# Sliding-window attention with a feed-forward behind it: the opening as one written list for all engines, keys loaded once a step

## The chip, the cores and the metric

The kernel runs on one core of a Trainium2 chip. The metric is the device time of the one launch in microseconds; lower is better.

## The reference

Attention over 4 batches, 8 heads, 768 tokens and 64 dimensions; a query sees the 8 global tokens and the 96 tokens up to itself, with a bias by distance. The attention's output, as 3072 tokens of 512 features, goes through a gated feed-forward without a nonlinearity.

```python
scores = scale * np.matmul(q, k.transpose(0, 1, 3, 2))
...
keep = is_global | is_local
dist = np.where(is_global & ~is_local, float(n_local), np.abs(rel))
bias = -slopes[:, None, None] * dist[None, :, :]
scores = np.where(keep, scores + bias, -1e9)
a = softmax(scores)
x = np.matmul(a, v)
...
a = x @ w1                      # 512 -> 1024
b = x @ w2
h = a * b @ w3                  # 1024 -> 1024
return h @ w_out                # 1024 -> 512
```

The inputs are float32; the weights come as 64-bit floats, which the kernel converts itself.

## The kernel before

*Weights.* `w3 @ w_out` is folded into one 1024x512 matrix on the chip: `fold(f, k)` (L135) adds one of 8 x 8 products, each two TensorE instructions, to the product for row block f. The result is split into a high and a low part (`wh` at L145, `wl` at L148). `w1` and `w2` are split likewise, 16 pieces (`w12`, L549; high part at L124, low part at L132). The 40 pieces of 512 KB (16 of `w3t`, 8 of `w_out`, 16 of `w1` and `w2`) come as 64-bit words into raw buffers (`stage`, `stage_xh`, `stage_xl`, `raws`) and are made to 32-bit words by three VectorE operations each (L56, L58, L60). `weights(...)` (L99) issues the loads of one or two pieces on SP's queue and converts them interleaved.

*Attention.* A step s is 128 queries of one batch and all heads, 24 steps, six to a batch. `load_keys` (L393) brings four overlapping windows of keys, 96 + 32 local and 8 global ones for each block of 32 queries, and the queries; `load_values` (L400) the values. Both tiles have one buffer. `scores` (L415) makes 32 small matmuls into the PSUM tile `sc`; `rows` (L428) takes the row maximum on VectorE (L435) and the exponential with its sum on ScalarE (L436); `probabilities` (L445) scales (L455 on ScalarE in steps 0 to 3, L458 on VectorE later) and transposes in 32x32 blocks (L461) into `pt`; `values` (L463) multiplies `pt` with the values by 64 small matmuls (32 in the first step of a batch) into the first 128 columns of `sc`; `tokens` (L502) splits the result into `xh` and `xl` (L65, L66).

*Feed-forward.* `run` (L150) is a generator for one unit of tokens, 256 for the first two units and 512 for the other five. It yields after about six matmuls, a slice; a unit of 512 tokens has 48 slices, one of 256 has 24. `gh` and `gl`, the gated product in two parts, use the buffers that hold `wo` and the raw pieces before.

*Order.* TensorE follows the program's order everywhere. The opening, `first_steps` (L515: the weights, steps 0 to 3 and the first slices), gives VectorE and SP their order too, while ScalarE's order there is the planner's. From step 4 on TensorE and ScalarE follow the program and VectorE and SP the planner. There a step is `visit(s)` (L493: `values(s - 1)`, `scores(s)`, and the loads), the rows with one slice behind each of the four query blocks, `tokens(s - 1)`, two slices, `probabilities(s)` and the other slices, 12 from step 8 on. A unit of 512 tokens is put behind the waiting work by `tokens`.

Of the kernel before, what the change touches and what calls it, by code (L numbers as in the profile page):

```python
# [45 lines left out]


def convert(nc, pieces):


    for dst, raw, src in pieces:
        nc.sync.dma_start(out=dst if src.dtype == F32 else raw, in_=src.bitcast(I32))
    pieces = [(dst, raw.rearrange("p (n t) -> p n t", t=2)) for dst, raw, src in pieces if src.dtype != F32]

    for dst, w in pieces:
        nc.vector.tensor_scalar(out=dst, in0=w[:, :, 1], scalar1=3, scalar2=0x3FFFFFF8, op0=ALU.logical_shift_left, op1=ALU.bitwise_and)  # L56
    for dst, w in pieces:
        nc.vector.scalar_tensor_tensor(out=dst, in0=w[:, :, 1], scalar=-0x40000000, in1=dst, op0=ALU.bitwise_and, op1=ALU.bitwise_or)  # L58
    for dst, w in pieces:
        nc.vector.scalar_tensor_tensor(out=dst, in0=w[:, :, 0], scalar=29, in1=dst, op0=ALU.logical_shift_right, op1=ALU.bitwise_or)  # L60
# [8 lines left out]
class FeedForward:  # L69
# [25 lines left out]
    def next(self, ring, slots):
        self.turn[ring] += 1
        return slots[(self.turn[ring] - 1) % len(slots)]

    def weights(self, *names):  # L99


        pieces, fresh = [], []
        for kind, *at in names:
            if kind == "w":
                f, n = divmod(at[0], 2)

                raw = self.stage[{3: 0, 5: 2, 6: 0}[f] + n] if f in (3, 5, 6) else self.raws[:, n]
                dst, src = self.t3s[:, at[0] % 4], self.src[n][f]
                fresh.append((n, f, dst.bitcast(F32).rearrange("p (i m) -> p i m", i=NCC)))
            elif kind == "o":  # L110
                dst, src = self.wo[:, at[0]], self.w_out[at[0]]
            else:
                f, z = at
                dst = self.mp.tile([P, PC], I32, tag=self.next(0, "agagoo"), name=f"t3_{f}_{z}")
                src = self.w3t[f, :, z * PC:(z + 1) * PC]
                self.t3[f, z] = dst
            if kind != "w":
                raw = self.next(1, self.stage + self.first)
            pieces.append((dst, raw, src))
# [533 lines left out]
```

## Time and profile before

| what | us |
|---|---|
| median of three runs | 596.34 (594.66 to 597.28) |
| the profiled execution | 594.8 |
| its span, first to last instruction | 592.9 |
[...]

The span is what the trace shows; the rest of the profiled execution's time lies around it. Busy times count an engine's instructions; consecutive matmuls overlap, so the time of a run of matmuls is read from the pitch between starts and not from the duration of one.

### The profile page before, as it was taken

Reading aid. Unit: us, or ns where it says so; the run is one execution under the profiler, and the core shown is the slowest. Engines: PE = TensorE matmul, PEld = TensorE weight load, DVE = VectorE, ACT = ScalarE, POOL = GpSimd, SP = SyncE. Lnnn points to the kernel's source line nnn. Section 1 sums busy time; section 2 is a strip of 40 time slices with the busy share of each in tenths; the row PEclk is TensorE's granted clock in tenths of the full one; section 3 lists DMA queues with packets and bytes.
Section 4 is the critical chain, followed back from the end, with each engine's and each line's share of the span. In section 5 each row is a group of like instructions: output and inputs, shape, how many; then the busy total and the mean of one; then the engine's idle time right before and its main releaser. Section 6 shows DMA issues by size and latency. Waiting matters only on the chain.

```text
span 592.9 us, 14620 instructions
## 1 busy us (share of the span) xinstructions
PE 538.7 (91%) x6400; PEld 423.2 (71%) x6400; DVE 273.6 (46%) x788; ACT 187.0 (32%) x591; POOL 2.9 (0%) x20
## 2 busy tenths in 40 slices
PE   2959597979999799999999998999979999999995
PEld 0424254977998588887877787888867878888884
DVE  7759687885354343533355413535233454112200
ACT  2032533544243243233324322433232343112210
POOL 1000000000000000000000000000000000000000
PEclk9979978989999899999999999999999999999999
DMA  8678554732144242134213322231342131100011
GB/s 288 250 278 295 221 192 161 271 130 72 49 141 167 92 130 92 44 106 148 86 46 128 132 94 108 73 112 48 119 166 66 65 130 38 55 18 1 1 37 40
DMA packets 17881, 69.52 MB, mean 117 GB/s; under 512 B 1936, under 2 KB 3984, under 8 KB 15248
## 3 DMA queue, kind: packets, MB, share of 16 engines
q1 hardware_dynamic: 17808, 68.49, 32.5%
q8 instruction: 52, 0.85, 0.6%
q14 instruction: 21, 0.17, 0.1%
HBM read 62.20 MB, written 6.29 MB: 116 GB/s over the span
## 4 chain that ended last, share of the span: by engine, by line
PE 74%; DVE 13%; ACT 5%; DMA 4%; issue 2%; SPq 1%; ACTq 0%; DVEq 0%
PE m L163 14%; PE m L162 14%; PE m L164 14%; PE o L179 7%; PE o L181 7%; PE o L180 7%; PE sc L478 6%; PE sc L426 4%; ACT pr L436 2%; PE w L143 2%; DVE pt L461 1%; ACT pr L455 1%; DVE t3s L58 1%; DMA stage<-w 1%; DMA stage_xh<-w_out 1%
## 5 line engine op out<-in xcount | busy, mean ns | idle before, releaser
L436 ACT ACTIVATE pr<-pr,mx 128x136 f32<-128x136 f32 (+2 forms) x192 | 74.2, 388 | 83.0 <-DVE mx L435 83.0
L162 PE MATMUL m<-xh,w1h 128*128 128x512 f32 (+1 forms) x224 | 82.4, 368 | 6.4 <-ACT xh L65 6.4
L172 DVE TENSOR_TENSOR g<-m,a 128x512 f32<-128x512 f32 x48 | 33.0, 688 | 110.7 <-PE m L164 110.7
L163 PE MATMUL m<-xl,w1h 128*128 128x512 f32 (+1 forms) x224 | 81.7, 365 | 2.1 <-DVE xl L66 2.1
L164 PE MATMUL m<-xh,w1l 128*128 128x512 f32 (+1 forms) x224 | 81.1, 362 | 0.0
L162 PE MATMUL m<-xh,w2h 128*128 128x512 f32 (+1 forms) x224 | 80.7, 360 | 0.0
L164 PE MATMUL m<-xh,w2l 128*128 128x512 f32 (+1 forms) x224 | 80.4, 359 | 0.0
L163 PE MATMUL m<-xl,w2h 128*128 128x512 f32 (+1 forms) x224 | 80.3, 359 | 0.0
L143 PE MATMUL w<-wo,t 128*128 128x512 f32 x128 | 61.2, 636 | 17.8 <-DVE wo L60 17.4
L179 PE MATMUL o<-wh,gh 128*128 128x512 f32 x192 | 76.0, 396 | 0.3 <-ACT gh L65 0.3
L181 PE MATMUL o<-wh,gl 128*128 128x512 f32 x192 | 74.9, 390 | 0.0
L180 PE MATMUL o<-wl,gh 128*128 128x512 f32 x192 | 74.8, 390 | 0.0
L65 ACT ACTIVATE gh<-g 128x512 fp32r<-128x512 f32 x48 | 30.3, 632 | 125.6 <-DVE g L172 125.6
L143 PEld LDWEIGHTS w<-wo,t 128*128 128x128 f32 x128 | 25.5, 205 | 51.0 <-issue 28.0
L435 DVE CUSTOM_DVE_ANT_0 pr<-sc,biasw 128x136 f32<-128x136 f32 x160 | 37.0, 295 | 50.5 <-PE sc L426 50.5
L478 PEld LDWEIGHTS sc<-pt,vr 32*64 32x64 f32 x2816 | 40.8, 140 | 24.8 <-DVE pt L461 17.5
L478 PE MATMUL sc<-pt,vr 32*64 32x32 f32 (+3 forms) x2816 | 44.5, 260 | 14.7 <-DVE pt L461 14.7
L162 PEld LDWEIGHTS m<-xh,w1h 128*128 128x128 f32 x224 | 42.6, 190 | 16.1 <-ACT xh L65 8.1
L163 PEld LDWEIGHTS m<-xl,w1h 128*128 128x128 f32 x224 | 42.7, 191 | 9.5 <-DVE xl L66 3.4
L164 PEld LDWEIGHTS m<-xh,w1l 128*128 128x128 f32 x224 | 42.7, 191 | 6.4
L162 PEld LDWEIGHTS m<-xh,w2h 128*128 128x128 f32 x224 | 42.3, 189 | 6.9 <-issue 0.4
L163 PEld LDWEIGHTS m<-xl,w2h 128*128 128x128 f32 x224 | 42.3, 189 | 6.3
(82 smaller groups left out, 563.6 us busy)
## 6 DMA issues: line engine op xcount, KB each, us to landing
qr<-qk SPq DMA_DIRECT2D x20, 1344.0 KB, 6.6
vr<-vx SPq DMA_DIRECT2D x20, 512.0 KB, 3.8
stage<-w3t SPq DMA_DIRECT2D x15, 512.0 KB, 7.6
out_dram<-ot SPq DMA_DIRECT2D x24, 256.0 KB, 2.0
raws<-w SPq DMA_DIRECT2D x10, 512.0 KB, 7.1
stage<-w SPq DMA_DIRECT2D x6, 512.0 KB, 9.0
qr<-qk SPq DMA_DIRECT2D x4, 528.0 KB, 5.0
stage_xh<-w_out SPq DMA_DIRECT2D x4, 512.0 KB, 8.0
```

The source lines that it names most:

```text
L65: nc.scalar.activation(hi, x, AF.Copy)
L143: nc.tensor.matmul(ps, lhsT=self.t3[f, z][:, i * P:(i + 1) * P].bitcast(F32), rhs=self.wo[:, k].bitcast(F32), start=k == 0, stop=k == NFC - 1)
L162: nc.tensor.matmul(ps[:, z], lhsT=mh, rhs=xh[:, i], start=i == 0, stop=False)
L163: nc.tensor.matmul(ps[:, z], lhsT=mh, rhs=xl[:, i], start=False, stop=False)
L164: nc.tensor.matmul(ps[:, z], lhsT=ml, rhs=xh[:, i], start=False, stop=i == NCC - 1)
L172: nc.vector.tensor_tensor(out=g, in0=ps, in1=a, op=ALU.mult)
L179: nc.tensor.matmul(ps, lhsT=gh[:, f, ts], rhs=self.wh[:, f], start=f == 0, stop=False)
L180: nc.tensor.matmul(ps, lhsT=gh[:, f, ts], rhs=self.wl[:, f], start=False, stop=False)
L181: nc.tensor.matmul(ps, lhsT=gl[:, f, ts], rhs=self.wh[:, f], start=False, stop=f == NFC - 1)
L435: nc.vector.tensor_tensor_reduce(out=x, in0=sc[scored(u, q, w0, w1)], in1=bias, scale=-SCALE, scalar=3.0e38, op0=ALU.add, op1=ALU.min, acc ...
L436: nc.scalar.activation(x, x, AF.Exp, bias=m, scale=-1.0, accum_out=sm[:, q, u:u + 1])
L478: nc.tensor.matmul(sc[cols, hp, q0 * R:q1 * R], lhsT=v[rows, i, cols], rhs=of(pt[rows], u), start=n == 0, stop=n == len(parts) - 1, skip_g ...
```

## The change

One list, `ORDER`, gives the opening for TensorE, VectorE, ScalarE and SP, up to the end of step 7 and of the first feed-forward unit, which now has 512 tokens like the other five. Each entry is an operation and its place. `d` issues a load (t: a piece of `w3t`, o: of `w_out`, w: of `w1` or `w2`, q and v: keys and values of a step). `A`, `B`, `C` are the three conversions of a piece; `wh`, `wl` the high and low part of a piece of `w1` or `w2`; `F` a fold; `ph`, `pl` the parts of a folded block. `S`, `R`, `E`, `s`, `c`, `X`, `V`, `h`, `l` are a step's scores, maxima, exponentials, sums, scaling, transpose, values, and the two parts of its output. `U`, `a`, `g`, `gh`, `gl`, `Z`, `ot` are unit 0: half of a first product, its copy, the gated product and its two parts, a quarter of a second product, and the store. Four more raw buffers are added and given out by `fetch` in the order in which they came free.

The keys of a step are loaded once: 128 of the window, the 8 globals, and the other 96, so that each query block reads 136 columns in a row, the globals among them. The values have the same order. Both tiles have two buffers. The bias tables are made with fewer VectorE and more ScalarE operations. From step 8 on the loop issues a step's maxima, exponentials, slices, transposes and slices, then its values, the next step's scores, and the two parts of its output.

```diff
-KW = NR * KF
+KW = WIN + GLB + P
-NV = 2 * NR - 1
+NV = 2 * NR
+LATE = 4
+STEPS = 8
+FIRST = 5
+SLICES = [4] * 9 + [8] * (B * NB - 9)
+ORDER = """
+d.t30 nt d.t00 d.q0 A.t30 B.t30 d.t20 bias d.o1 S.0 d.o0 A.t00 B.t00 C.t00 d.q2 C.t30 A.o1 B.o1 d.t41 A.o0 B.o0 d.t01 C.o0 C.o1 F.0.0 d.o2 A.t20 B.t20
+d.o5 R.0.0 F.3.0 R.0.1 E.0.0 R.0.2 d.t31 E.0.1 R.0.3 A.t01 E.0.2 F.0.1 A.o2 d.v0 B.o2 E.0.3 F.3.1 d.t60 A.o5 B.t01 s.0 d.o4 C.t20 c.0 C.t01 F.2.0 d.o6
+A.t31 B.o5 F.2.1 C.o2 d.t10 X.0.0 F.0.2 d.t11 X.0.1 F.3.2 A.o6 V.0 d.q1 B.o6 C.o6 F.2.2 A.t10 A.o4 d.o3 B.t10 h.0 l.0 C.t10 S.1 C.o5 B.t31 A.o3 F.1.0
+d.q3 C.t31 R.1.0 F.1.1 R.1.1 E.1.0 R.1.2 F.1.2 E.1.1 R.1.3 B.o3 S.2 E.1.2 C.o3 E.1.3 B.o4 F.0.3 d.q4 s.1 C.o4 F.1.3 c.1 F.0.4 d.t51 F.3.3 d.t50 F.0.5
+X.1.0 F.3.4 X.1.1 d.v1 A.t11 F.0.6 R.2.0 d.w4 F.3.5 R.2.1 E.2.0 A.t50 F.2.3 d.t21 E.2.1 B.t50 V.1 C.t50 d.v2 R.2.2 R.2.3 E.2.2 d.o7 A.t51 S.3 B.t11
+E.2.3 C.t11 d.v3 h.1 F.3.6 l.1 d.w7 s.2 F.1.4 c.2 A.o7 B.o7 F.1.5 C.o7 F.1.6 B.t51 d.w14 F.0.7 X.2.0 F.1.7 d.t40 A.t21 ph.0 X.2.1 F.3.7 ph.1 pl.0 V.2
+pl.1 ph.3 B.t21 C.t21 A.t40 F.2.4 d.t71 h.2 C.t51 l.2 F.5.0 d.w0 pl.3 F.2.5 B.t40 C.t40 F.5.1 A.t71 d.t70 F.2.6 B.t71 A.w0 F.5.2 C.t71 F.2.7 B.w0 d.w5
+C.w0 F.5.3 ph.2 A.t70 d.w2 wh.0 F.4.0 pl.2 B.t70 F.5.4 C.t70 F.4.1 A.t41 d.w1 B.t41 F.7.0 C.t41 F.5.5 A.w2 B.w2 F.7.1 C.w2 F.5.6 A.w1 wh.2 F.7.2 B.w1
+C.w1 F.5.7 wl.2 wh.1 F.7.3 R.3.0 ph.5 F.4.2 R.3.1 E.3.0 pl.5 F.7.4 E.3.1 R.3.2 F.4.3 R.3.3 E.3.2 wl.1 S.4 E.3.3 A.w5 B.w5 F.7.5 s.3 C.w5 c.3 F.4.4
+A.t60 d.w11 B.t60 F.7.6 C.t60 d.w3 F.4.5 wl.0 wh.5 X.3.0 F.6.0 d.v4 X.3.1 F.7.7 d.t61 A.w4 F.6.1 ph.7 A.w3 V.3 B.w3 pl.7 C.w3 R.4.0 wh.3 F.6.2 A.t61
+d.v5 E.4.0 wl.3 F.4.6 h.3 A.w7 l.3 F.6.3 B.w7 U.0.0.0 C.w7 B.t61 wh.7 d.w13 F.4.7 C.t61 U.0.0.1 R.4.1 ph.4 E.4.1 pl.4 F.6.4 wl.7 A.w11 U.0.1.0 R.4.2
+R.4.3 E.4.2 F.6.5 B.w11 E.4.3 C.w11 U.0.1.1 s.4 wh.11 d.w6 B.w4 c.4 F.6.6 C.w4 U.1.0.0 wl.11 d.w8 wl.5 F.6.7 wh.4 X.4.0 U.1.0.1 ph.6 X.4.1 a.0 pl.6
+V.4 a.1 g.0 A.w6 gh.0 B.w6 U.1.1.0 C.w6 gl.0 wh.6 d.w9 wl.6 U.1.1.1 wl.4 A.w8 U.2.0.0 g.1 A.w9 gh.1 B.w9 U.2.0.1 gl.1 B.w8 U.2.1.0 a.2 C.w8 C.w9 wh.8
+d.w12 wh.9 U.2.1.1 wl.8 d.w15 wl.9 U.3.0.0 g.2 d.q6 A.w13 gh.2 A.w12 U.3.0.1 B.w12 d.q5 A.w15 C.w12 U.3.1.0 a.3 B.w15 d.w10 wh.12 C.w15 U.3.1.1 B.w13
+wh.15 C.w13 S.5 g.3 wh.13 A.w10 gh.3 B.w10 U.4.0.0 C.w10 gl.2 wh.10 U.4.0.1 wl.10 A.w14 U.4.1.0 a.4 B.w14 C.w14 gl.3 wh.14 U.4.1.1 R.5.0 R.5.1 E.5.0
+U.5.0.0 g.4 E.5.1 R.5.2 R.5.3 gh.4 U.5.0.1 E.5.2 gl.4 wl.13 S.6 E.5.3 wl.12 a.5 s.5 U.5.1.0 c.5 X.5.0 U.5.1.1 X.5.1 U.6.0.0 g.5 R.6.0 gh.5 R.6.1 E.6.0
+U.6.0.1 gl.5 R.6.2 E.6.1 R.6.3 U.6.1.0 a.6 wl.15 E.6.2 wl.14 h.4 U.6.1.1 E.6.3 l.4 V.5 g.6 s.6 gh.6 c.6 U.7.0.0 h.5 d.v7 gl.6 l.5 X.6.0 d.v6 Z.0.0
+d.q7 X.6.1 U.7.0.1 d.q8 Z.0.1 a.7 U.7.1.0 Z.0.2 U.7.1.1 V.6 g.7 gh.7 gl.7 S.7 h.6 Z.0.3 R.7.0 R.7.1 E.7.0 R.7.2 Z.1.0 ot.0 R.7.3 E.7.1 l.6 S.8 E.7.2
+E.7.3 Z.1.1 s.7 c.7 Z.1.2 X.7.0 Z.1.3 X.7.1 V.7 ot.1 Z.2.0 h.7 l.7 Z.2.1 Z.2.2 Z.2.3 Z.3.0 ot.2 Z.3.1 Z.3.2 Z.3.3 ot.3
+"""
...
+    def fetch(self, kind, *at):
+
+        late = kind == "w" and at[0] >= LATE
+        r = 0 if late or not self.free[1] or self.free[0] and self.since[0][0] <= self.since[1][0] else 1
+        raw = self.free[r].pop(0)
...
+        self.nc.sync.dma_start(out=to, in_=src.bitcast(I32))
...
+    def convert(self, part, kind, *at):
...
+        elif part == 0:
+            v.tensor_scalar(out=dst, in0=raw[:, :, 1], scalar1=3, scalar2=0x3FFFFFF8, op0=ALU.logical_shift_left, op1=ALU.bitwise_and)
+        elif part == 1:
+            v.scalar_tensor_tensor(out=dst, in0=raw[:, :, 1], scalar=-0x40000000, in1=dst, op0=ALU.bitwise_and, op1=ALU.bitwise_or)
+        else:
+            v.scalar_tensor_tensor(out=dst, in0=raw[:, :, 0], scalar=29, in1=dst, op0=ALU.logical_shift_right, op1=ALU.bitwise_or)
...
+class Unit:
...
+    def first(self, f, n, half):
+
+        if half == 0:
+            self.ps[f, n] = self.ff.ps.tile([P, self.width], F32, tag="m", name=f"m_{self.c}_{f}_{n}")
+        ps, (xh, xl) = self.ps[f, n], self.x
+        for i in range(half * NCC // 2, (half + 1) * NCC // 2):
+            mh, ml = (w[:, f, i] for w in self.ff.w[n])
+            self.nc.tensor.matmul(ps, lhsT=mh, rhs=xh[:, i], start=i == 0, stop=False)
+            self.nc.tensor.matmul(ps, lhsT=mh, rhs=xl[:, i], start=False, stop=False)
+            self.nc.tensor.matmul(ps, lhsT=ml, rhs=xh[:, i], start=False, stop=i == NCC - 1)
...
     def load_keys(s):
         b, t = divmod(s, NB)
-        k0 = 0 if t else OWN
-        q = at.tile([P, NP, QW], F32, tag="qr", name=f"qr_{s}")
+        k0 = 0 if t else WIN
+        q = at.tile([P, NP, QW], F32, tag="qr", bufs=2, name=f"qr_{s}")
...
+        v = at.tile([P, NV, P], F32, tag="vr", bufs=2, name=f"vr_{s}")
...
     def frame(s, q):
 
-        return (0, KF) if s % NB else (WIN - R * q, P)
+        return (0 if s % NB else WIN - R * q), KF
...
-            k0 = q * KF if s % NB else OWN - w0
+            k0 = q * R
...
+        blocks = sorted(range(0 if s % NB else NR - 1, NV), key=lambda i: i != NR)
+        for n, i in enumerate(blocks):
+            q0, q1 = max(0, i - NR), min(NR, i + 1)
...
+        if s % 4 == 3:
+            units[s // 4] = Unit(ff, s // 4, xh, xl, (s - 3) * P)
+            work.append(units[s // 4].run())
...
+    do = dict(A=lambda *x: ff.convert(0, *x), B=lambda *x: ff.convert(1, *x), C=lambda *x: ff.convert(2, *x), wh=ff.high, wl=ff.low, F=ff.fold, ph=ff.fold_high, pl=ff.fold_low, S=scores, R=maxima, E=exponentials, s=sums, c=lambda s: scale(s, nc.scalar if s < FIRST else nc.vector), X=turn, V=values, h=high, l=low, bias=biases, biasA=lambda: None, nt=sizes)
...
-    SLICES = [0] * 3 + [10] * 3 + [8] * 2 + [12] * (n - 8)
     with tc.manual_schedule(engines={mybir.EngineType.PE}):
-        with tc.manual_schedule(engines={mybir.EngineType.DVE, mybir.EngineType.SP}):
-            first_steps()
+        with tc.manual_schedule(engines={mybir.EngineType.DVE, mybir.EngineType.SP, mybir.EngineType.Activation}):
+            ordered()
+        work.append(units[1].run())
         with tc.manual_schedule(engines={mybir.EngineType.Activation}):
-            for s in range(4, n):
-                visit(s)
-                all_rows(s, lambda: slices(1))
-                tokens(s - 1)
-                slices(2)
-                probabilities(s, nc.vector)
-                slices(SLICES[s] - NR - 2)
-            visit(n)
-            tokens(n - 1)
+            for s in range(STEPS, n):
+                load(s)
+                if s + 1 < n:
+                    keys(s + 1)
+                for q in range(NR):
+                    maxima(s, q)
+                    exponentials(s, q)
+                    slices(1)
+                slices(SLICES[s] // 2)
+                sums(s)
+                scale(s, nc.vector)
+                turn(s, 0)
+                turn(s, 1)
+                slices(SLICES[s] - SLICES[s] // 2)
+                values(s)
+                if s + 1 < n:
+                    scores(s + 1)
+                high(s)
+                low(s)
             slices(10 ** 6)
...
-    nc = bacc.Bacc("TRN2", target_bir_lowering=False, num_devices=1)
+    nc = bacc.Bacc("TRN2", target_bir_lowering=False, num_devices=1, dynamic_dma_scratch_size=1024)
```

## Rows read from the trace of the kernel before

**Rows 1.** The profile's page, busy time and share of the span of each engine (PE = TensorE matmul, PEld = its weight loads, DVE = VectorE, ACT = ScalarE).
```profile
PE 538.7 (91%) x6400; PEld 423.2 (71%) x6400; DVE 273.6 (46%) x788; ACT 187.0 (32%) x591; POOL 2.9 (0%) x20
```

**Rows 2.** Busy time by stretch: stretch and its length in us, busy us of each engine (instructions), granted TensorE clock as a share of 2.4 GHz, busy share of the 16 DMA engines, GB/s.
```profile
0.00:40.00 40.00, 22.17 (x103) 9.33 (x104) 27.45 (x76) 5.27 (x17) 2.93 (x20) 0.92 0.80 291
40.00:100.00 60.00, 49.45 (x469) 24.66 (x475) 46.42 (x114) 24.51 (x82) 0.00 (x0) 0.90 0.60 222
100.00:140.00 40.00, 35.48 (x553) 33.04 (x539) 33.09 (x92) 19.19 (x58) 0.00 (x0) 0.93 0.41 150
140.00:187.40 47.40, 47.14 (x778) 42.29 (x784) 22.51 (x76) 17.57 (x63) 0.00 (x0) 1.00 0.34 116
```

**Rows 3.** Waits of PE: the first two rows are those of 0 to 187.4 us, the last three those of 187.4 us to the end. Engine, tile, line, what it waited for: us in total, times, longest.
```profile
PE w L143 <- DVE wo L60: 17.4, 2, 10.6
PE sc L478 <- DVE pt L461: 14.7, 5, 7.1
...
PE sc L426 <- issue: 6.4, 5, 1.6
PE m L162 <- ACT xh L65: 6.4, 4, 2.7
PE m L163 <- DVE xl L66: 2.1, 4, 1.4
```

**Rows 4.** The chain that ended last, in order of time: start us, us, what. L478 is the start of `values`, and so of a `visit`.
```profile
187.38 1.74 PE sc L478 x87
...
210.31 1.74 PE sc L478 x88
...
229.73 1.74 PE sc L478 x88
...
268.56 1.74 PE sc L478 x88
...
289.81 0.95 PE sc L478 x52
...
308.45 1.74 PE sc L478 x87
...
350.50 1.74 PE sc L478 x87
...
371.99 1.74 PE sc L478 x88
...
429.24 1.74 PE sc L478 x88
...
452.72 1.74 PE sc L478 x88
...
514.12 1.74 PE sc L478 x88
...
586.89 0.60 ACT ot L185
```

**Rows 5.** The timeline of PE: start us, us, instruction. The first row is 32 fold instructions; the other two are the first and the last of 69 feed-forward matmuls in a row, so 68 pitches apart.
```profile
53.44 14.00 PE L143 MATMUL w<-wo,t 128*128 128x512 f32 x32
...
334.69 0.39 PE L179 MATMUL o<-wh,gh 128*128 128x512 f32 x1
...
350.11 0.39 PE L181 MATMUL o<-wh,gl 128*128 128x512 f32 x1
```

**Rows 6.** The timeline of DVE in the opening: the first operation of a weight piece that is converted by itself, then that of the next group, of two interleaved pieces, and that of the group behind it.
```profile
8.64 0.42 DVE L56 TENSOR_SCALAR wo<-stage 128x512 int32<-128x512 int32 x1
...
10.43 0.76 DVE L56 TENSOR_SCALAR t<-stage 128x512 int32<-128x512 int32 x2
...
13.51 0.76 DVE L56 TENSOR_SCALAR wo<-stage_xh 128x512 int32<-128x512 int32 x2
```

**Rows 7.** The timeline of DVE in visit 8: the first and the last of the eight row maxima (one each 0.22 us), the sums, the scaling, the subtraction of `tokens`, the two transposes.
```profile
190.31 0.30 DVE L435 CUSTOM_DVE_ANT_0 pr<-sc,biasw 128x136 f32<-128x136 f32 x1 [4.24 <-PE sc L426]
...
191.86 0.30 DVE L435 CUSTOM_DVE_ANT_0 pr<-sc,biasw 128x136 f32<-128x136 f32 x1
...
195.42 0.17 DVE L448 TENSOR_SCALAR sm<-sm 128x8 f32<-128x8 f32 x1 [3.26 <-ACT pr L436]
...
195.86 1.29 DVE L458 TENSOR_TENSOR pr<-pr,sm 128x1088 f32<-128x1088 f32 x1
197.07 0.68 DVE L66 TENSOR_TENSOR xl<-sc,xh 128x512 fp32r<-128x512 f32 x1
197.67 1.56 DVE L461 STREAM_TRANSPOSE pt<-pr 128x640 f32<-128x640 f32 x2
```

**Rows 8.** Short stretches of the opening, columns as in rows 2: the DMA engines as they start, when full, in the wait for `wo`, and among smaller transfers.
```profile
4.00:6.00 2.00, 0.00 (x0) 0.00 (x0) 1.76 (x9) 0.00 (x0) 0.00 (x0) 1.00 0.93 274
8.00:10.00 2.00, 0.00 (x0) 0.00 (x0) 1.90 (x4) 1.99 (x5) 0.00 (x0) 1.00 1.03 422
34.00:36.00 2.00, 0.00 (x0) 0.00 (x0) 1.03 (x3) 0.00 (x0) 0.00 (x0) 0.50 1.01 410
44.00:46.00 2.00, 2.00 (x6) 0.93 (x5) 0.65 (x1) 2.00 (x8) 0.00 (x0) 1.00 0.78 283
```

**Rows 9.** The page's DMA issues: of two loads, issuing queue, count, size of one, median us from issue to landing.
```profile
qr<-qk SPq DMA_DIRECT2D x20, 1344.0 KB, 6.6
vr<-vx SPq DMA_DIRECT2D x20, 512.0 KB, 3.8
```

More of the change, by code (lines that the diff above doesn't have):

```diff
@@ L45 @@
 SCALE = 1.0 / 8.0
[L48 to L60, printed above, removed]
 def split(nc, hi, lo, x):
@@ L95, in next @@
[L95 to L103, printed above, removed]
+        raws = xp.tile([P, 2, 2 * PC], I32, tag="xl", name="raws")
+        more = bp.tile([P, 2, 2 * PC], I32, name="more_raws")
+        self.raws = [x[:, i] for x in (raws, more) for i in range(2)]
+        self.free = [self.raws, self.stage]
+        self.since = [[0] * len(x) for x in self.free]
@@ L110, in weights @@
             elif kind == "o":
-                dst, src = self.wo[:, at[0]], self.w_out[at[0]]
+                dst = self.wo[:, at[0]]
             else:
[L113 to L119, printed above, removed]
@@ new lines, in convert, with high, low @@
+        if part == 2:
+            self.freed += 1
+            self.free[piece[3]].append(piece[2])
+            self.since[piece[3]].append(self.freed)
+    def high(self, i):
+        f, n = divmod(i, 2)
+        self.nc.scalar.activation(self.w[n][0][:, f], self.t3s[:, i % 4].bitcast(F32).rearrange("p (i m) -> p i m", i=NCC), AF.Copy)
+    def low(self, i):
+        f, n = divmod(i, 2)
+        hi, lo = (w[:, f] for w in self.w[n])
+        self.nc.vector.tensor_tensor(out=lo, in0=self.t3s[:, i % 4].bitcast(F32).rearrange("p (i m) -> p i m", i=NCC), in1=hi.bitcast(F32), op=ALU.subtract)
@@ L183, in run @@
+        for t in range(self.width // P):
+            for j in range(NFC // 2):
+                self.second(t, j)
+                if j < NFC // 2 - 1:
                     yield
-            o = mp.tile([P, DO], F32, tag="o", name=f"ot_{c}_{t}")
-            nc.scalar.activation(o, ps, AF.Copy)
-            nc.sync.dma_start(out=self.out[bass.ds(row + t * P, P), :], in_=o)
+            self.store(t)
             yield
@@ L426, in scores, with maxima, exponentials @@
                     nc.tensor.matmul(sc[hp * R:(hp + 1) * R, i, cols], lhsT=m[rows, hp, KW + q * R:KW + (q + 1) * R], rhs=m[rows, hp, k0 + w0:k0 + w1], start=True, stop=True)
-    def rows(s, q):
+    def maxima(s, q):
+        if q == 0:
+            stats[s] = [at.tile([P, NR, 2], F32, tag=t, bufs=2, name=f"{t}_{s}") for t in ("mx", "sm")]
+        w0, w1 = frame(s, q)
+        for u in range(2):
+            bias = (biasw if s % NB else bias0)[:, u, q, w0:w1]
+            nc.vector.tensor_tensor_reduce(out=pr[:, q, u, w0:w1], in0=sc[scored(u, q, w0, w1)], in1=bias, scale=-SCALE, scalar=3.0e38, op0=ALU.add, op1=ALU.min, accum_out=stats[s][0][:, q, u:u + 1])
+    def exponentials(s, q):
         w0, w1 = frame(s, q)
@@ new lines, in ordered @@
+    def ordered():
+        ff.more_stages(xp, bp)
+        for name in ORDER.split():
+            name, *args = name.split(".")
+            if name in "dABC":
+                kind, *digits = args[0]
+                if kind == "w":
+                    digits = ["".join(digits)]
+                args = [kind, *map(int, digits)]
+            else:
+                args = [int(x) for x in args]
+            if name != "d":
+                do[name](*args)
+            elif kind in "qv":
+                (keys if kind == "q" else load)(*args[1:])
+            else:
+                ff.fetch(*args)
+        work.clear()
```

341 lines of the change are left out of this document (130 added, 211 removed).

## The prediction

> **What bounds the kernel now.** I read the page's engine sums first, then the stretches, the waits of TensorE (PE), and the chain. PE is busy for 91% of the span and no other engine for half of it [rows 1]; so the time is PE's work plus PE's gaps, and the question is where the gaps are. The stretches [rows 2] answer it: from 140 us on PE is all but full; before that it is busy for 22.2 us of 40, then 49.5 of 60, then 35.5 of 40, at a lower granted clock. In the same stretches VectorE (DVE) is busy for 27.5, 46.4 and 33.1 us: it converts weights, and PE waits for them. The waits [rows 3] name it: up to 187.4 us PE stood 17.4 us for a converted `wo` piece (10.6 of it the start) and 14.7 us for `pt`, the transposed probabilities. After that it still stands 6.4 us "issue" inside `scores` and 6.4 + 2.1 us for the `xh` and `xl` of a new feed-forward unit.
>
> The chain [rows 4] times the later loop, since each `values` piece opens a `visit`. A clean visit is 210.31 to 229.73, 19.42 us. Twelve slices of six 512-column matmuls, at a pitch of (350.11 - 334.69)/68 = 0.2268 us [rows 5], are 16.33; so `values` and `scores` together cost 3.09. Visit 8 began at 187.38; with its pair and two slices (2.72) that finish the second 256-token unit, the state "scores of step 8 done, 512 tokens through the feed-forward" is reached at 193.2.
>
> From there, without any gap, PE would need: 240 slices, 1440 x 0.2268 = 326.6; 15 pairs, 46.4, less 2 x 0.78 for the two steps that begin a batch (289.81 to 308.45 is 18.64); the last `values`, 1.74; and 6.0 from the last matmul to the end (586.89 to 592.9). That is 379.2, and 193.2 + 379.2 = 572.4. The real end is 592.9, so the loop loses 20.5 us. Visits 8, 12, 16 and 20, where one unit ends and the next wants `xh` at once, run over by 6.2 (22.93 against 3.09 and ten slices), 1.8, 2.1 and 4.1 [rows 4]; one issue wait of 1.6 is in the last. So 12.6 us are unit boundaries, 6.4 issue waits, 1.5 small things.
>
> **The loop from step 8.** It runs the same slices: 8 in step 8, 12 in each later one, 52 behind the last `values`; 240. Two things differ. `high(s)` and `low(s)` stand right behind `values(s)`, ahead of the next exponentials. And unit 0 is finished in the list, so unit 1 starts level with step 8 and still has 4 slices left when unit 2 is appended, and so on. Those 5.4 us of PE work cover the 1.3 us of one ScalarE copy and one DVE subtraction (0.68, [rows 7]). I cost the boundary waits at zero, a gain of 12.6; without that cover they are back. The two short steps get 40 matmuls in `values` for 32, some 0.25 us each: +0.5. The loop then needs 379.7 and its issue waits.
>
> `values(s)` comes 12 slices, 16.3 us, behind `scores(s)`, as now. In visit 8 the maxima start at 190.31 and the second transpose ends 8.9 us later [rows 7]. DVE's order in the loop is not written out; at worst it takes the sums behind all of the first eight slices (10.9), a product (0.7), then 0.44 + 1.21 + 1.56: 14.8, still in time. I cost it at nothing.
>
> **Keys and values.** `qr` falls from 1344 KB [rows 9] to 128 x 4 x 360 x 4 B = 720 KB, and both tiles get two buffers. In the loop PE waits for no load [rows 3], so this is worth nothing there; it shortens the transfers of the opening.
>
> **The issue waits.** 6.4 us in five visits of sixteen, always in `scores` right behind `values`. The loop keeps that order of the same small matmuls, so I keep 6.4 (bounds 0 and 12.8). [...]
>
> **The opening list** decides. I sum each engine's entries of `ORDER` at the trace's pitches.
>
> PE: 64 folds of two instructions at 14.00/32 = 0.4375 [rows 5], 56.0; 48 half-units (`U`, `Z`) of 6 x 0.2268, 65.3; eight pairs of 3.09 less 2 x 0.54, 23.6. Sum 145.
>
> DVE: a weight piece by itself takes 1.79 us (8.64 to 10.43), two interleaved take 3.08 (10.43 to 13.51) [rows 6]. The list has 40 pieces and 46 places where an operation directly follows the one that it needs: 40 x 1.54 + 46 x 0.12 = 67. Then, from [rows 7]: 64 maxima at 0.22, 14; 16 transposes at 0.78, 12.5; 48 subtractions and products at 0.60, 29; eight sums and three scalings, 7; the bias, now 8 operations for 16 on at most 168 columns, 2 to 3. Sum 132.
>
> Three cuts bound the end of the list from below. (a) PE: F.0.0 needs o0, the sixth large transfer, 3.2 MB in. The engines moved 274 GB/s at 4 to 6 us and 410 to 422 when full [rows 8], so it lands near 12; conversion makes that 14.5; 14.5 + 145 = 159. (b) DVE: its first data come near 4, 132 of work, and 12.7 of PE work stand behind the last transpose: 149. (c) Transfers: F.0.7 needs o7, 15.9 MB in. At 410 GB/s that lands at 43, is converted at 45, and 115 of PE work follow: 160. At the 283 GB/s of 44 to 46 us [rows 8] it lands near 59: 176.
>
> So nothing forces the list beyond 160, while the present opening comes to the same state at 193.2 with as much PE work; 193 is the upper bound, all its waits kept. Between them I take 169. Near the end of the weights the sums of DVE and PE run level in the list (85 and 80 at wl.4, 112 and 108 at wl.14), so that each of the 16 tiles of w1 and w2 may hold PE for one DVE operation in flight: 16 x 0.6 = 10 on top of 159. I stay near the cuts because the waits of [rows 3] lose their cause: the last `wo` pieces now are ordinary entries with eight raw buffers, not a transfer queued behind a `vr` load that waits for `values`; and between a step's maxima and its `values` the list puts folds or half-units. What could hold it: SP takes its transfers in written order, so that one without a free raw buffer holds those behind it, later the stores of unit 0 and `vr` of step 8 too (needed 10.9 us after the list ends; a `vr` lands in 3.8 [rows 9]). The bias has ten more ScalarE instructions, at most 0.6 us each by the 512-wide copy at 586.89 [rows 4]; ScalarE was busy 5.3 of the first 40 us [rows 2], and if that did not hide them, the first exponentials come 6 us later, with folds beside them.
>
> **Sum.** 169 + 379.7 + 6.4 = 555.1 of span; 1.9 lie around the span (594.8 against 592.9): 557.0. The profiled execution is 1.5 below the median shown, so 557 stands for either.
>
> **The rivals.**
>
> *The opening keeps its waits.* In-order queues on four engines convoy: a late piece holds DVE, that holds PE. For it: the level sums, little slack. Against it: none of the cuts is tight for long. At 193: 581.
>
> *The clock.* When PE stood for `wo`, the granted clock was 0.50 at 34 to 36 us [rows 8], the lower level. [...] Against it: the clock fell behind a wait of 6.8, and the list shows no such hole. [...]
>
> *The boundaries come back* in the loop, because a unit's start waits elsewhere (a buffer of `gh`, a PSUM tile): 557 + 12.6 = 570.
>
> *The change does nothing for PE*: waits only move, in opening and loop: 593 to 597.
>
> *Slower.* One mechanism: DVE's unwritten order puts sums, scaling and transposes so late that `values(s)` stalls in every step. It begins to cost above 16.3 us from `scores`, against 8.9 now and 14.8 at worst by my count; each us beyond costs 15. To end above 599 it takes 19.1 us in every step. PE would then show waits for `pt` in the loop, of which [rows 3] have none.
>
> **Chances.** Forecast, 546 to 568: 0.64. Opening keeps its waits, or the clock, 568 to 585: 0.20. Boundaries back, near 570: 0.06. No change: 0.04. Slower: 0.05. Below 546: 0.01. From 546, which is cut (a) with all else, to 582 the range holds 0.82. Faster by over 0.5% (about what a measurement can tell from no change) 0.91, within 0.04, slower 0.05.
>
> **What would show it.** The fourth store ends the list: near 170 us if right, 193 if the first rival holds. The loop: visits of 19.4 us at steps 12, 16, 20 too, no PE wait for `xh` behind 170 us, issue waits of 4 to 8 us in all. Opening: PE's waits for `wo` past the first and for `pt` nearly gone; granted clock above 0.9 to 100 us. A `qr` load is 720 KB and its traffic 12.8 MB less (20 x 624 KB). I am wrong if PE stands on DVE for more than 20 us between 15 and 170 us, or if PE waits for `pt` in the loop.

## The result, and the profile after

The changed kernel takes 579.72 us, the median of four runs (579.53 to 583.23), against 595.9 for the kernel before beside it: a ratio of 0.974, interval 0.971 to 0.978. It is faster, as forecast, and inside the range of 546 to 582, but the gain is 16 us where 39 were forecast. The profiled execution took 583.23, 3.5 above the median. The lines below are its lines, with a span of 581.4.

The page's lines on the engines, the DMA queue that brings instructions (packets, MB, share of 16 engines) and the key loads:
```profile
PE 534.8 (92%) x6272; PEld 411.3 (71%) x6272; DVE 275.5 (47%) x779; ACT 196.5 (34%) x609; POOL 4.0 (1%) x26
...
q8 instruction: 51, 0.84, 0.6%
...
qr<-qk SPq DMA_DIRECT2D x20, 720.0 KB, 5.6
```
TensorE (PE) still is the one engine that fills the span, now for 92% [rows 1]; a key load has shrunk to 720 KB [rows 9], as worked out.

Busy time by stretch, columns as in [rows 2]:
```profile
0.00:40.00 40.00, 20.91 (x268) 10.29 (x272) 28.37 (x83) 16.13 (x58) 3.97 (x26) 0.91 0.77 288
40.00:100.00 60.00, 53.46 (x656) 26.16 (x640) 45.18 (x112) 23.01 (x75) 0.00 (x0) 0.94 0.59 206
100.00:140.00 40.00, 37.56 (x333) 28.69 (x333) 35.52 (x81) 19.96 (x51) 0.00 (x0) 1.00 0.40 138
140.00:187.40 47.40, 45.62 (x690) 37.08 (x690) 25.07 (x90) 17.88 (x63) 0.00 (x0) 1.00 0.32 110
```
Against [rows 2], PE is busy for 4 us more between 40 and 100 us and for 2 more in the next stretch; in the first 40 it is not, and it is still idle for 19 us there.

The waits of PE; the first six rows are those of 0 to 187.4 us, the last is the only one behind it:
```profile
PE sc L487 <- DMA qr<-qk: 14.9, 3, 9.5
PE w L167 <- DVE wo L147: 4.3, 1, 4.3
PE sc L487 <- issue: 3.3, 1, 3.3
PE w L167 <- DVE t L147: 3.0, 3, 2.4
PE sc L487 <- DVE mx L496: 1.8, 3, 1.1
PE sc L539 <- DVE xl L567: 1.2, 1, 1.2
...
PE sc L487 <- issue: 10.4, 9, 1.6
```
The 14.7 us for `pt` of [rows 3] are gone and those for `wo` are down from 17.4 to 4.3. No row is a wait for a part of `w1` or `w2`. Of the 14.9 for keys (`qr`), 9.5 are the start. In the loop the waits for `xh` and `xl` are gone and the issue waits have grown from 6.4 to 10.4.

The chain of work, of the list's end and of the loop; L539 begins `values`, L487 `scores`:
```profile
173.63 1.74 PE sc L539 x88
...
199.10 0.83 PE sc L487 x40
199.93 0.98 issue
...
339.56 1.74 PE sc L539 x88
...
362.52 1.74 PE sc L539 x88
```
The list ends 12.6 us behind the start of the last `values` in it (1.74, and eight slices of six matmuls): 173.6 + 12.6 = 186.3, where the forecast had 169 and the kernel before 193.2. The loop takes 581.4 - 186.3 = 395.1 where 386.1 were forecast. So 17.3 us of the miss of 26.3 are in the opening and 9.0 in the loop. In the loop nine of sixteen visits run over their 19.42, all with an issue wait in `scores` like the one at 199.93, by 15.2 us together. 10.4 of these are the waits themselves. The visit at 339.56 takes 22.96, 3.54 too many with a wait of 1.60. The two visits that begin a batch take 18.88, the 18.64 of before and the 0.25 that the forecast added.

### The profile page after: what moved, and what is told of

Read it like the earlier page. It is cut to its first block, busy times and chain, and to the rows that moved or that the text cites. A ratio compares the mean times of both kernels' runs of the same rounds, so it can differ in the third digit from the quotient of the medians.

```text
span 581.4 us, 14382 instructions
## 1 busy us (share of the span) xinstructions
PE 534.8 (92%) x6272; PEld 411.3 (71%) x6272; DVE 275.5 (47%) x779; ACT 196.5 (34%) x609; POOL 4.0 (1%) x26
## 4 chain that ended last, share of the span: by engine, by line
PE 75%; DMA 10%; DVE 9%; issue 3%; ACT 1%; SPq 0%; ACTq 0%
PE m L192 13%; PE m L193 13%; PE m L194 13%; PE o L220 8%; PE o L221 7%; PE o L222 7%; PE sc L539 6%; PE sc L487 5%; PE w L167 2%; DMA stage<-w 2%; DMA raws<-w_out 2%; DMA more_raws<-w 1%; DMA qr<-qk 1%; DMA vr<-vx 1%; DVE t3s L147 1%
## 5 line engine op out<-in xcount | busy, mean ns | idle before, releaser
L192 PE MATMUL m<-xh,w1h 128*128 128x512 f32 x192 | 77.3, 402 | 0.4 <-ACT xh L562 0.4
L192 PE MATMUL m<-xh,w2h 128*128 128x512 f32 x192 | 75.7, 394 | 0.0
L193 PE MATMUL m<-xl,w1h 128*128 128x512 f32 x192 | 75.0, 391 | 0.2 <-DVE xl L567 0.2
L194 PE MATMUL m<-xh,w1l 128*128 128x512 f32 x192 | 74.8, 390 | 0.0
L194 PE MATMUL m<-xh,w2l 128*128 128x512 f32 x192 | 74.7, 389 | 0.0
L193 PE MATMUL m<-xl,w2h 128*128 128x512 f32 x192 | 74.7, 389 | 0.0
L487 PE MATMUL sc<-qr 64*32 64x136 f32 (+3 forms) x1536 | 33.3, 288 | 30.7 <-DMA qr<-qk 14.9
L167 PEld LDWEIGHTS w<-wo,t 128*128 128x128 f32 x128 | 26.0, 211 | 38.6 <-issue 26.4
L487 PEld LDWEIGHTS sc<-qr 64*32 64x32 f32 x1536 | 23.1, 111 | 37.9 <-issue 16.6
L539 PEld LDWEIGHTS sc<-pt,vr 32*64 32x64 f32 x2880 | 38.5, 130 | 11.9 <-issue 6.7
L198 ACT ACTIVATE a<-m 128x512 f32<-128x512 f32 x48 | 28.5, 594 | 51.4 <-PE m L194 51.2
L212 DVE TENSOR_TENSOR gl<-g,gh 128x512 fp32r<-128x512 f32 x48 | 33.1, 690 | 22.6 <-ACT gh L207 22.3
L220 PEld LDWEIGHTS o<-wh,gh 128*128 128x128 f32 x192 | 36.4, 189 | 9.3 <-issue 1.9
```

The source lines that it names most:

```text
L167: self.nc.tensor.matmul(self.prod[f], lhsT=self.t3[f, z][:, i * P:(i + 1) * P].bitcast(F32), rhs=self.wo[:, k].bitcast(F32), start=k == 0, ...
L192: self.nc.tensor.matmul(ps, lhsT=mh, rhs=xh[:, i], start=i == 0, stop=False)
L193: self.nc.tensor.matmul(ps, lhsT=mh, rhs=xl[:, i], start=False, stop=False)
L194: self.nc.tensor.matmul(ps, lhsT=ml, rhs=xh[:, i], start=False, stop=i == NCC - 1)
L212: self.nc.vector.tensor_tensor(out=self.gl[:, f], in0=self.g[f], in1=self.gh[:, f].bitcast(F32), op=ALU.subtract)
L220: self.nc.tensor.matmul(ps, lhsT=self.gh[:, f, ts], rhs=ff.wh[:, f], start=f == 0, stop=False)
```

## Experiments

Each is the changed kernel with one edit or, where it is said, with several; times are medians, to be set against 579.7. The kernel before, run beside them, took 594.8 to 595.9, so differences of less than 1 us are not read.

### The loop: what are the issue waits?

**Apart.** Two slices are put between the two bursts of small matmuls.
```diff
-                slices(SLICES[s] - SLICES[s] // 2)
+                slices(SLICES[s] - SLICES[s] // 2 - 2)
                 values(s)
+                slices(2)
                 if s + 1 < n:
                     scores(s + 1)
```


> In the loop of the changed kernel two of the twelve slices of a step stand between values(s) and scores(s+1), where the two came back to back. Theory A: the issue waits (10.4 us of PE, nine steps, about 12 us of time) come because the 384 PE instructions of values and scores are used up faster than instructions are fetched; with 24 large instructions between the two they go: issue waits under 2 us, 566 to 569 us against 579.7. Rival: any boundary of fetched instructions that falls in scores costs its 1.3 us wherever scores stands: 8 to 11 us of issue waits stay, 578 to 581 us.

**Loads later.** The loop's loads are issued behind the four query blocks, in a written order, away from the end of `scores`.
```diff
-        with tc.manual_schedule(engines={mybir.EngineType.Activation}):
+        with tc.manual_schedule(engines={mybir.EngineType.Activation, mybir.EngineType.SP}):
...
-                load(s)
-                if s + 1 < n:
-                    keys(s + 1)
                 for q in range(NR):
                     maxima(s, q)
                     exponentials(s, q)
                     slices(1)
+                load(s)
+                if s + 1 < n:
+                    keys(s + 1)
```


> In the loop the loads of values and of the next keys are issued behind the four query blocks of a step, SP in the program's order, so that no load is under way while values(s) and scores(s+1) run; those two stay back to back. Theory A (density alone): nothing changes, 9 to 11 us of issue waits, 578 to 581 us. Rival (traffic): the fetch is slow because the 512 KB load that starts as values ends fills the DMA engines; then the issue waits fall under 4 us and the time is 568 to 573 us.

Apart: 571.38, ratio 0.960 (0.958 to 0.962). Loads later: 580.26, ratio 0.974 (0.973 to 0.976). All waits of PE in the loop, of the first and of the second:
```profile
PE sc L539 <- DVE pt L526: 1.0, 1, 1.0
```
```profile
PE sc L487 <- issue: 10.6, 9, 1.6
```
The first has no issue wait left, as theory A has it, though its 566 to 569 us were too low. Its clean visit takes 19.65 instead of 19.42, 3.5 us over fifteen visits, and 8.3 us are gained all the same. The second has nine waits, and they stand where those of the changed kernel stand, behind 40, 31, 23, 45, 37, 28, 42, 34 and 25 of the 64 instructions of `scores`, though other loads now run beside them. So it is not the traffic of these loads.

The places move by 8 or 9 from one step to the next. By the trace, where each small matmul of the program is two instructions, a step has 72 matmuls in slices, 128 in `values` and 64 in `scores`, 264, each with a weight load: 528 instructions; a step that begins a batch has 432. The larger instruction queue on the profile's page (q8) has packets of 0.84 MB / 51 = 16.5 KB, and 31 of the 51 come from 197.36 to 502.38 us. The fifteen visits of that time have 13 x 528 + 2 x 432 = 7728 PE instructions, so a packet holds some 249 of them and a step takes about two packets; that is an estimate, which counts all of q8 and nothing else as PE's. If the waits of one step and of the next stand two packets apart, their moves of 8 or 9 matmuls make these two packets 528 less 16 to 18 instructions, 255 or 256 each. If the count sets the place of these waits, more instructions ahead of the loop shift them.

**Phase.** Step 8 gets eleven slices instead of eight, 18 matmuls more ahead of the next `scores`.
```diff
-SLICES = [4] * 9 + [8] * (B * NB - 9)
+SLICES = [7] * 9 + [8] * (B * NB - 9)
```


> The changed kernel with 11 slices in step 8 in place of 8: one slice of reserve at a unit's end is left of four, and all later PE instructions stand 36 earlier in every later step. Theory A, sharpened (which instruction of scores is the last of a fetched block decides: stalls stood at the 23rd to the 45th of its 64 matmuls, and at none below): the nine stalls move 18 matmuls down, to 22, 13, 5, 27, 19, 10, 24, 16 and 7, so three issue waits or four stay, in steps 8, 13 and 19, 4 to 5 us; 570 to 573 us. Rival (the run without reserve was faster for another reason, as its unit starts): 578 to 581 us, nine waits.

571.18, ratio 0.960 (0.956 to 0.964). Its waits in the loop, and where they stand (x is the number of `scores` instructions from the wait on, of 64):
```profile
PE sc L487 <- issue: 3.5, 3, 1.3
```
```profile
204.32 0.92 PE L487 MATMUL sc<-qr 64*32 64x136 f32 x42 [1.31 <-issue]
302.12 0.89 PE L487 MATMUL sc<-qr 64*32 64x136 f32 x37 [1.09 <-issue]
419.33 0.90 PE L487 MATMUL sc<-qr 64*32 64x136 f32 x40 [1.11 <-issue]
```
Three waits, behind 22, 27 and 24 instructions: 40, 45 and 42 less 18, as expected; their 3.5 us are a little under the 4 to 5. The six others would have come 18 earlier too, behind 5 to 19, and none is there. So the count of instructions sets the place.

The count also says which places cost time. It gives a place in `scores` to other visits too. In those that begin a batch, where `values` has 80 matmuls for 128, it is about 54 and 51 in the changed kernel and 36 and 33 here, and none of them has a wait. A place counted from the start of `values` sorts all of them: the waits of the changed kernel and of this one stand behind 150 to 173 small matmuls in a row, and the places without one come at 148 at most. That such a packet is late because small matmuls are used up faster than it arrives fits with this and with "apart", where large matmuls between the bursts removed all nine; it is argued, since no row here shows which instructions a packet brings.

**No reserve.** Step 8 keeps its twelve slices, so that a unit is used up when the next is appended, as in the kernel before.
```diff
-SLICES = [4] * 9 + [8] * (B * NB - 9)
+SLICES = [8] * (B * NB)
```


> Step 8 takes 12 slices in place of 8, so that a unit ends exactly with a step and the next one begins with the next step's first slice, without four slices of reserve. If the reserve is what removed the waits at unit boundaries, PE waits for xh or xl at steps 12, 16, 20 and behind the last step again: 1.0 to 1.5 us each, 583 to 586 us with the clock's share. If the earlier place of the two parts behind values is enough, those waits are under 0.5 us each and the time is 578 to 581.

573.94, ratio 0.963 (0.961 to 0.965): 5.8 us less than the changed kernel, which neither theory had. Its waits in the loop:
```profile
PE m L192 <- ACT xh L562: 2.8, 4, 0.7
PE sc L487 <- issue: 1.3, 1, 1.3
PE m L193 <- DVE xl L567: 0.9, 4, 0.2
```
The boundary waits are back, at four boundaries and for 3.7 us: that is what the reserve saves here, where the two parts of the output already stand right behind `values`. But the edit also puts 24 matmuls more ahead of the next `scores`, and that phase leaves one issue wait of nine, behind 22 instructions where 45 less 24 is 21. Each edit of the loop's length has that second effect, which must be taken off before it is read.

### The opening: what holds the list?

Where the 17 us are is read from the starts of `values` on PE's timeline. "PE's work" is the list's own at the trace's pitches; V.0 and the end are times in the span, the other columns us from one start to the next.

| | V.0 at | V.0 to V.1 | to V.2 | to V.3 | to V.4 | to V.5 | V.5 to end | end at |
|---|---|---|---|---|---|---|---|---|
| PE's work | | 15.0 | 9.2 | 27.6 | 16.9 | 34.4 | 34.4 | |
| changed kernel | 29.0 | 20.1 | 16.3 | 28.8 | 18.3 | 38.6 | 35.2 | 186.3 |
| queries' order | 26.6 | 21.4 | 10.6 | 29.0 | 18.3 | 38.4 | 35.2 | 179.5 |
| half the bytes | 26.4 | 17.0 | 10.3 | 27.8 | 17.1 | 38.6 | 35.2 | 172.4 |
| two operations | 25.3 | 20.1 | 10.4 | 27.3 | 18.0 | 35.5 | 35.2 | 171.8 |

The profiled execution of the changed kernel is late at V.0: in the four runs of the loop above, which have the same opening, V.0 comes at 26.4 to 27.0, V.2 36.7 to 38.6 us behind it, and the list ends at 184.7 to 185.9.

Between V.0 and V.2 the changed kernel takes 12 us more than its work. SP's timeline shows the queue there (start, us the issue took):
```profile
16.67 7.38 SPq L123 DMA_DIRECT2D more_raws<-w_out  x2
...
26.28 0.38 SPq L458 DMA_DIRECT2D qr<-qk  x1
29.59 0.33 SPq L123 DMA_DIRECT2D more_raws<-w_out  x1
36.39 4.69 SPq L458 DMA_DIRECT2D qr<-qk  x2
41.18 0.37 SPq L123 DMA_DIRECT2D stage<-w3t  x1
```
A pair of issues at 16.67 takes 7.4 us, held for a free raw buffer, and the keys of step 1, three loads behind, go out at 26.28 only; PE waits 2.95 us for them, up to 34.23. The keys of steps 3 and 4 need the buffers that S.1 and S.2 free: the first go out at 36.39, when S.1 has ended (34.23 + 2.07), and the second when S.2 has, and the weight pieces behind them start at 41.18. Between 29.92 and 36.39 SP issues nothing at all. The DMA engines in that time, then in the rush behind it, and in what followed (columns as in [rows 2]):
```profile
32.00:36.00 4.00, 1.77 (x64) 1.62 (x64) 2.01 (x5) 0.00 (x0) 0.00 (x0) 0.73 0.17 68
36.00:40.00 4.00, 4.00 (x57) 1.77 (x46) 3.97 (x20) 3.20 (x16) 0.00 (x0) 0.84 0.58 189
...
52.00:56.00 4.00, 0.85 (x35) 0.56 (x35) 1.54 (x3) 0.96 (x6) 0.00 (x0) 0.79 1.03 394
56.00:60.00 4.00, 3.85 (x33) 1.87 (x34) 1.92 (x5) 1.48 (x4) 0.00 (x0) 0.50 0.11 44
```
From 32 to 36 us the engines are busy for 0.17, in the middle of the weights. At 52 they are full, and there the issue wait in S.3 takes 3.3 us where those of the loop take 1.6 at most; behind it the granted clock is 0.50.

**Queries' order.** Three loads are moved in the list, so that each comes when its buffer is free or nearly so: step 1's keys earlier, those of steps 3 and 4 later.
```diff
-... d.v0 B.o2 ... V.0 d.q1 B.o6 ... F.1.0 d.q3 C.t31 ... F.0.3 d.q4 s.1 ... d.w4 F.3.5 ... d.v2 R.2.2 ...
+... d.v0 d.q1 B.o2 ... V.0 B.o6 ... F.1.0 C.t31 ... F.0.3 s.1 ... d.w4 d.q3 F.3.5 ... d.v2 d.q4 R.2.2 ...
```


> In the list three key loads are moved on SP's queue: q1 up behind v0, q3 down behind w4, q4 down behind v2, so that no weight piece stands behind a key load that waits for scores. Theory B (the opening is held by the written order of the queue, with the DMA engines idle meanwhile at 32 to 44 us): the engines stay full there, scores of step 1 no longer waits 3 us, and the list ends 5 to 10 us earlier: 570 to 575 us. Rival (the opening is held by the bytes or by DVE and PE themselves): within 2 us, 578 to 581.

574.24, ratio 0.964 (0.962 to 0.967): 5.5 us less, as theory B has it. The first two stretches are those that stood at 0.17 and 0.58, the third that of S.3:
```profile
32.00:36.00 4.00, 3.91 (x67) 2.46 (x68) 3.98 (x17) 0.80 (x4) 0.00 (x0) 0.50 0.77 270
36.00:40.00 4.00, 4.00 (x69) 1.88 (x67) 3.38 (x12) 3.46 (x18) 0.00 (x0) 0.72 0.89 318
...
48.00:52.00 4.00, 2.94 (x191) 2.66 (x192) 2.16 (x11) 1.68 (x8) 0.00 (x0) 1.00 0.30 101
```
The engines are now busy there, and S.3 has no issue wait. V.1 to V.2 falls from 16.3 to 10.6. V.1 itself does not come closer behind V.0: S.1 no longer waits for keys, but 3.2 us for VectorE's `l.0` (in the row below), which stands behind conversions of weight pieces; and the clock is at 0.50 in the first of these stretches. PE's longest waits up to 180 us:
```profile
PE sc L487 <- DMA qr<-qk: 11.9, 2, 9.6
...
PE sc L487 <- DVE xl L567: 3.4, 2, 3.2
```

**Half the bytes, two operations.** On top of it, one kernel loads half of each weight piece, another converts a piece with two of the three VectorE operations. The first leaves out half of the weights' words and sets that half to zero once, on GpSimd; the second leaves out the sign and the top bit of the exponent.
```diff
+        for x in self.raws + self.stage:
+            self.nc.gpsimd.memset(x[:, PC:], 0)
...
-        self.nc.sync.dma_start(out=to, in_=src.bitcast(I32))
+        self.nc.sync.dma_start(out=to[:, :PC], in_=src.bitcast(I32)[:, :PC])
```


> The kernel with the three key loads moved, but only half of each weight piece is loaded (the rest is zeros), 10 MB less; all conversions and matmuls stay. If arrival of data still holds the list: 5 to 10 us less than 574.2, so 564 to 569 us. If VectorE, TensorE and the waits between them hold it: 572 to 575 us.


```diff
         elif part == 1:
-            v.scalar_tensor_tensor(out=dst, in0=raw[:, :, 1], scalar=-0x40000000, in1=dst, op0=ALU.bitwise_and, op1=ALU.bitwise_or)
+            pass
```


> The kernel with the three key loads moved, but each of the 40 weight pieces is converted with two VectorE operations of three (the sign and the top exponent bit are left out), 40 x 0.6 = 24 us less of VectorE; loads and matmuls stay. If the hand-over from VectorE to TensorE holds the list, as the forecast's 10 us on top of the cut say: 8 to 15 us less than 574.2, 559 to 566 us. If TensorE's own work and the data's arrival hold it: 571 to 575 us.

567.68, ratio 0.954 (0.951 to 0.957), and 568.65, ratio 0.959 (0.955 to 0.964): 6.6 and 5.6 us less than 574.24. The first is what "arrival of data" had, the second lies between its two expectations. In the profiled executions the lists end 7.1 and 7.7 us earlier than with the queries' order alone. The table shows where. Of the 7.1, 4.4 lie between V.0 and V.1, where they bring PE to within 2.0 us of its work: PE's wait for `l.0` falls from 3.2 to 0.9 us, and the granted clock from 32 to 40 us is 1.00 where it was 0.50 and 0.72. Of the 7.7, 2.9 lie between V.4 and V.5, where the last pieces of w1 and w2 are converted beside unit 0 and PE comes from 4.0 to 1.1 us of its work; 1.3, 1.3 and 1.7 come up to V.0, up to V.1 and between V.2 and V.3. So the bytes cost most at the beginning, and VectorE's operations all along the list up to V.5. The two were not tried together. From V.5 on nothing that was tried changes anything: there PE alone sets the time.

### Both together

**Order and apart.** The edits of "queries' order" and "apart" in one kernel.

> Both moves that helped in one kernel: two slices between values and scores in the loop, and the three key loads moved on SP's queue in the list. They act in different stretches, so their gains should add: 579.7 - 8.3 - 5.5, 565 to 567 us, with no issue wait behind 190 us. If one's gain is given back in the other's stretch: 569 to 571.

566.43 (564.83 to 566.79), ratio 0.953 (0.950 to 0.956), 13.3 us below the changed kernel and the fastest of this study. The gains add, as expected: 8.3 + 5.5 = 13.8.

**A further order.** On top of it, the keys of step 5 are loaded much earlier, and S.1 and one fold come earlier on PE.
```diff
-... F.2.2 A.t10 ... l.0 C.t10 S.1 C.o5 ... V.1 C.t50 ... h.1 F.3.6 l.1 ... d.w3 F.4.5 ... B.w12 d.q5 A.w15 ...
+... F.2.2 S.1 A.t10 ... l.0 C.t10 C.o5 ... V.1 F.3.6 C.t50 ... h.1 l.1 ... d.w3 d.q5 F.4.5 ... B.w12 A.w15 ...
```


> The kernel with both moves, and three more places in the list: the load of q5 up behind w3 (scores of step 5 waited 2.2 us for it), scores of step 1 ahead of the split of step 0 (it waited 3.2 us for the subtraction that stands behind conversions on VectorE), one fold between the values of step 1 and the scores of step 3. If the list is TensorE's work plus these waits, each taken wait comes off the end: 4 to 6 us less than 566.4, 560 to 563 us. If another wait ends just behind each of them: 565 to 568 us.

569.25, ratio 0.955 (0.951 to 0.959): 2.8 above, with intervals that overlap, so it is no gain, and a loss is likely and not certain; neither expectation had that. SP's timeline, the VectorE operation that takes that last piece, and PE's waits:
```profile
82.82 0.42 SPq L458 DMA_DIRECT2D qr<-qk  x1
...
83.76 0.52 SPq L123 DMA_DIRECT2D stage<-w3t  x1
```
```profile
93.70 0.43 DVE L143 TENSOR_SCALAR t<-stage 128x512 int32<-128x512 int32 x1 [3.56 <-DMA stage<-w3t]
```
```profile
PE m L193 <- DVE xl L567: 3.7, 1, 3.7
...
PE sc L487 <- DVE mx L496: 2.6, 2, 2.2
```
The wait of S.5 for its keys went. But the load now stands ahead of the piece t61 (and of a `vr` load between them), VectorE waits 3.56 us for that piece, the subtraction `l.3` stands behind it in the list, PE waits 3.7 for the subtraction, and S.5 now waits 2.2 for a maximum (`mx`). One late transfer passed through three queues in their written order.

## Why the prediction was right and wrong

**Wrong: the list's end, 169 and measured 186.3.** The step that failed is the hand-over term: 16 tiles by 0.6 us, 10 us on top of cut (a). In its place the list stands 27 us over cut (a), and no matmul waits for one of these tiles (a weight load does once, for 0.2 us). From V.4 to V.5, where the last of them are made, 4.2 are lost, and PE's longest waits there are these, the last row that of "two operations":
```profile
PE sc L487 <- DMA qr<-qk: 2.4, 1, 2.4
PE sc L539 <- DVE xl L567: 1.2, 1, 1.2
...
PE sc L487 <- DMA qr<-qk: 0.8, 1, 0.8
```
The load of these keys (step 5) stands on SP's queue behind the pieces w12 and w15, which are issued when conversions have freed raw buffers. So VectorE costs time there, 2.9 us of it by "two operations", but by way of the queue and not from tile to tile.

By the table the 27 us are 7.5 ahead of V.0 (14.5 and eight folds, 7.0, make 21.5), 12.2 from V.0 to V.2, 4.2 from V.4 to V.5 and 3.4 in the other stretches. By cause, some 16 are waits that the forecast gave no time: 5.4 for keys behind the start, 6.0 for VectorE's `t`, `mx` and `xl`, 3.3 of issue wait in S.3, 0.5 for values, and 0.7 that the first fold comes later than 14.5. Of the rest some 8, an estimate, are the clock (below). The forecast's own sign of being wrong, PE on DVE for more than 20 us, would not have caught it.

It named the hazard, that SP takes transfers in written order and one without a free buffer holds those behind it, and gave it no time, since each of the three cuts was slack by itself. "Queries' order" measures it at 5.5 us, from three loads. "Half the bytes" and "two operations" gain 6.6 and 5.6 us on top of that, though cuts (c) and (b) had put transfers and VectorE at 160 (176 at the lower rate) and 149: the cuts counted each engine as if it began its work when the list lets it. The first rival, that the opening keeps its waits, had the mechanism of the waits; it put the end at 193, and 186.3 lies nearer to it than to the forecast.

**Wrong: the issue waits, kept at 6.4.** They are 10.4, within the bounds of 0 and 12.8, and cost 15.2 with what follows them. The reason given, that the loop keeps the same small matmuls in the same order, is true and does not fix the number: the phase of the instruction count does, and "phase" and "no reserve" take it to 3.5 and 1.3. In the time of those fifteen visits, with 31 packets of instructions, PE has nine such waits, all among small matmuls and none among large ones: only some of the packets cost it time.

**Right: the boundaries.** 12.6 us were to go and went: no wait for `xh` or `xl` in the loop [rows 3]. The reserve of four slices has 3.7 of it by "no reserve"; that the new place of the two parts has the rest was not tried by itself.

**Right: the loop's own work.** Without waits 379.7 were worked out. "Apart" takes 569.6 less a list end of 184.9: 384.7, against 379.7 + 3.5 for its longer visits + 1.0 for its one wait for `pt`, 384.2.

**Right: `values` in time, and keys and values worth nothing in the loop.** PE waits for no load there and, in the changed kernel, never for `pt`; so the slower rival has no case. What the smaller key loads give in the opening was not tried by itself.

**The clock** does not do all that its rival made of it. The upper end of the range, 582, takes a granted clock of 0.50 all the way up to V.1, and no run shows that: in the changed kernel it is 0.91 up to 40 us and 0.94 from there to 100 (0.984 over the span, 0.975 before). The traces give it as a share of full speed, 1.00 or 0.50 at a time (here 0.50 in each us from 24 to 27, 1.00 in the next); that speed in GHz, as the line above [rows 2] has it, is shown by none. But the forecast gave the clock no time, and it took some. It fell behind waits: to 0.62 at 24 to 28 us, 0.73 and 0.84 at 32 to 40, 0.50 at 56 to 60, and for some 3 us at 345 in the loop. And the first fold instructions, by their weight loads, start (19.67 - 16.26)/4 = 0.853 us apart, the pitch that they have again at 25 us with a granted clock of 0.50, though the rows give 1.00 from 16 to 20 us:
```profile
16.26 0.34 PEld L167 LDWEIGHTS w<-wo,t 128*128 128x128 f32 x1 [0.52 <-issue]
...
19.67 0.34 PEld L167 LDWEIGHTS w<-wo,t 128*128 128x128 f32 x1 [0.52 <-issue]
```
The sixteen fold instructions ahead of V.0 take 6.13 + 5.30 = 11.4 us for 7.0; at 36 to 40 and 56 to 64 us and in S.1 (2.07 for 1.20) the lower clock takes some 4 more. These are the 8 us above, an estimate from these rows.

The two failed steps add up to the miss of the profiled execution, 17.3 + 9.0 = 26.3; that execution is 3.5 us above the median. Of the best kernel, the loop takes 384.4 (563.0 - 178.6) where 386.1 were forecast, but not by the forecast's terms: it has none of the 6.4 of issue waits and pays 3.5 for longer visits and 1.0 for `pt`. Its list is 9.6 over the forecast.

## What to carry to other kernels

A list for several in-order queues is not priced by each engine's sum: follow each blocking issue to what stands behind it on its queue, and on to the engine that waits for that, since the cuts can all be slack and still cost time one after the other. In this kernel's loop PE had issue waits only behind 150 or more small matmuls in a row; two slices of large ones between the two bursts removed all such waits, and gained 8.3 us after their price of 3.5. Where a change alters the number of instructions ahead of such a burst, read its result with the places of the issue waits beside it.
